# An mLSTM cell without its decay matrix: values divided by the decay, scores under a triangle

## The chip, the cores and the metric

The kernel runs on one core of one Trainium2 chip. Its time is device microseconds of one execution; the figure that counts is the median of several executions. Five engines work side by side and meet at semaphores: TensorE (PE in the profile, its weight loads apart as PEld), VectorE (DVE), ScalarE (ACT), GpSimd (POOL) and SyncE (SP), which here only issues DMAs. PE's results land in PSUM; POOL works on SBUF alone.

## The reference

An mLSTM cell over 4 batches, 8 heads, 768 tokens and head size 40, and then a dense pair of layers of 320 x 2048 and 2048 x 320 over the 3072 tokens, with g = h - tanh(h) between them.

```python
for t in range(S):
    m_new = np.maximum(f_gate[:, :, t] + m, i_gate[:, :, t])
    f_stab = np.exp(f_gate[:, :, t] + m - m_new)
    i_stab = np.exp(i_gate[:, :, t] - m_new)
    m = m_new
    C = f_stab * C + i_stab * outer(vt, kt)
    n = f_stab * n + i_stab * kt
    h_tilde = C @ qt
    denom = np.maximum(np.abs(n . qt), 1.0)
    y[:, :, t] = sigmoid(o_gate[:, :, t]) * h_tilde / denom
...
h = x @ w_in
g = h - np.tanh(h)
return (g @ w_out).astype(np.float32)
```

The forget gates are drawn as 3 + 0.5 x normal, the input gates as 0.5 x normal. `w_in` and `w_out` are float64 (a float32 array times a numpy float64), so each weight is 8 bytes in memory and is turned into float32 on the chip.

## The kernel before

**Units.** The 768 tokens are cut into 6 chunks of L = 128. A unit is one chunk of one batch with its 8 heads: 24 units, numbered chunk by chunk (unit n is chunk n // 4 of batch n % 4). Within a chunk the recurrence is written as attention. For each head PE multiplies keys and queries into scores (`score`, into the PSUM tile `ps`), DVE multiplies the scores by a decay matrix (L393, into `E`), and PE multiplies the result by the scaled values `vs` (`intra`, into `ph`). What comes from earlier chunks is added by `inter`: the queries times the decay since the chunk's start (`qg`) times the carried state. `update` forms the chunk's contribution to the state (`pc`), `gate` divides by the denominator and applies the output gate (`ys`), and `turn` transposes the unit's result into `xT`, the input of the dense layers. The denominator is a column of ones' product: `vs` carries exp(i - m) as its 41st column, so column D of `ph` is n . q.

**The decay matrix.** For each pair (s, t) of a chunk it holds the product of the forget factors between s and t. Each unit loads its 8 rows of forget factors from `f_rows`, spread over 128 partitions (`fetch`, a 512 KB DMA), and one scan over 128 x 1024 elements (L362) turns them, with `diag` as the added operand, into the products. `qg` comes from `g_rows`, the running product from the chunk's start, by two more DMAs, and POOL multiplies it by the queries (L378). Both tables of rows are made at the start: L233 to L242 compute exp of the log decays with a polynomial on DVE, PE transposes the result (L247), DVE scans it (L255), and ACT's queue writes both to memory (L258, L259).

**The start.** Two scans' worth of gate work on 32 rows (L203 to L208) gives m, the log decays `lf` and i - m. PE transposes `lf` and i - m into columns, and two matmuls over a triangle and over ones (L218 to L227) give the decay to the chunk's end (`eS`) and of a whole chunk (`eT`). `ei` holds exp(i - m), and that times `eS`.

**Weights.** 40 blocks of `w_in` and `w_out` (8 column pairs p, five blocks for each) are loaded as 8-byte words (L283) and turned into float32 by five DVE operations (L293, L296, L304, L305, L306) and two ACT operations (L294, L297). `convert` lists the steps; each p has a due time, the first dense item that needs it.

**Dense items.** Two units make a group g of 256 tokens; 12 groups and 8 pairs p make 96 items. `up` multiplies (12 recorded matmul passes into `ph_up`), ACT squares twice, DVE forms `gt` with two operations (L501, L502), and `down` of the item two places earlier multiplies by `w_out` (8 recorded passes into `po`). The first four groups are taken in parts, as `STAGES` says: an entry (g, first, last) runs pairs first to last of group g, and the number beside a list is how many cell slots are spread over it. Partial sums go to `part`.

**Cell slots.** A slot (s, o, x) is the scores of unit s, the value matmuls, update and gate of unit o, and the transpose of unit x, interleaved step by step. `begin` in a slot prepares unit o (`vs` on POOL), issues the loads for unit s + 1 and runs the decay scan for unit s. The first four slots run before the dense items, with the first nine conversion steps merged in. `kz` (keys) has two buffers, `q2` (queries) three.

**Order.** The order of PE's instructions is written by hand: class `T` chains each to the one before. The other engines are in the order that the framework gives them. All loads go through SP's queue, the outputs and the two tables of rows through ACT's.

**The branch.** The dense layers use a short polynomial for h - tanh(h), good while squares stay small. ACT adds up the squares in `sums`; at the end (L606 to L611) the maximum is compared with `TINY`, and only if it is larger, everything is computed a second time with a full formula.

Of the kernel before, what the change touches and what calls it, by code (L numbers as in the profile page):

```python
# [47 lines left out]
TINY = 0.0224  # L49

# [11 lines left out]
def kernel(  # L62
# [16 lines left out]
    class T:  # L79
# [60 lines left out]
    f_sb = att.tile([BH, S], FP, name="f_sb", tag="E", bufs=4)  # L140
    i_sb = att.tile([BH, S], FP, name="i_sb", tag="E", bufs=4)
# [7 lines left out]
    q2 = [const.tile([128, HH, L], FP, name=f"q2{i}") for i in range(3)]  # L149
    for t in (kz[0], q2[0], kz[1], q2[1], q2[2]):  # L150
        V.memset(t, 0.0)
# [3 lines left out]
    def load_unit(n):  # L155
        c, b = divmod(n, B)
        t = ld[n] = {"kz": kz[n % 2], "q2": q2[n % 3]}
        for i in range(2):
            r0, heads = i * D, slice(i, H, 2)
            nc.sync.dma_start(out=t["kz"][r0:r0 + D, heads], in_=kT[b, c, :, heads])  # L160
            nc.sync.dma_start(out=t["q2"][r0:r0 + D], in_=qT[b, c, :, heads])  # L161
        for name, src, bufs in (("v", v, 3), ("k", k, 4), ("o", o_gate, 4)):
            t[name] = load.tile([L, H, D], FP, name=name, tag=name, bufs=bufs)
            nc.sync.dma_start(out=t[name], in_=src[b, c])
# [5 lines left out]
    after = const.tile([128, 128], FP, name="after")  # L170
    ones = const.tile([128, TOP], FP, name="ones")
# [17 lines left out]

    G.memset(after, 1.0)  # L190
    G.affine_select(out=after, in_=after, compare_op=OP.is_ge, fill=0.0, base=-1,
                    pattern=[[-1, 128]], channel_multiplier=1)
    G.tensor_copy(out=diag, in_=ident.unsqueeze(1).to_broadcast([128, H, L]))
# [3 lines left out]
    ei = const.tile([L, 2, NT, BH], FP, name="ei")  # L197
# [3 lines left out]
    m_sb = att.tile([BH, S], FP, name="m_sb", tag="E", bufs=4)  # L201
    lf = att.tile([BH, S], FP, name="lf", tag="E", bufs=4)
    V.tensor_tensor_scan(out=m_sb, data0=f_sb, data1=i_sb, initial=-1.0e30, op0=OP.add, op1=OP.max)  # L203

    V.memset(lf[:, 0:1], 0.0)
    V.tensor_tensor(out=lf[:, 1:S], in0=f_sb[:, 1:S], in1=m_sb[:, 0:S - 1], op=OP.add)
    V.tensor_tensor(out=lf[:, 1:S], in0=lf[:, 1:S], in1=m_sb[:, 1:S], op=OP.subtract)
    V.tensor_tensor(out=i_sb, in0=i_sb, in1=m_sb, op=OP.subtract)  # L208

    def to_columns(row):  # L210
        p = ps_b.tile([L, NT, BH], FP, name="pcol", tag="b")
        for c in range(NT):
            T.transpose(p[:, c, :], row[:, c * L:(c + 1) * L], ident[0:BH, 0:BH])
        return p

    V.tensor_copy(out=lfT, in_=to_columns(lf))
    A.activation(out=ei[:, 0], in_=to_columns(i_sb), func=AF.Exp)
    for w in (after, ones):  # L218
        p = ps_b.tile([w.shape[1], NT, BH], FP, name="psum_lf", tag="b")
        T.matmul(p.rearrange("p c n -> p (c n)"), w, lfT.rearrange("p c n -> p (c n)"),  # L220
                 start=True, stop=True)
        if w is after:
            A.activation(out=eS, in_=p, func=AF.Exp)
            continue
        half = p.rearrange("p c (b j two) -> p (c b) two j", two=2, j=HH)
        A.activation(out=eT, in_=half[:, :, 1, :], func=AF.Exp)
        A.activation(out=eT[0:D], in_=half[0:D, :, 0, :], func=AF.Exp)  # L227
    V.tensor_tensor(out=ei[:, 1], in0=ei[:, 0], in1=eS, op=OP.mult)


    NR = NT * BH // 2
    xr, n, f = (mlp.tile([L, 2, NR], FP, name=name, tag=tag) for name, tag in (("xr", "z"), ("n", "z"), ("f", "q")))
    V.tensor_single_scalar(xr, lfT.rearrange("p (i c) n -> p i (c n)", i=2), -87.0, op=OP.max)  # L233
    V.tensor_scalar(out=n, in0=xr, scalar1=1.4426950408889634, scalar2=ROUND, op0=OP.mult, op1=OP.add)
    V.tensor_single_scalar(n, n, ROUND, op=OP.subtract)
    for part in LN2:
        V.scalar_tensor_tensor(out=xr, in0=n, scalar=-part, in1=xr, op0=OP.mult, op1=OP.add)
    V.tensor_single_scalar(f, xr, EXPO[0], op=OP.mult)
    for coef in EXPO[1:]:
        V.scalar_tensor_tensor(out=f, in0=f, scalar=coef, in1=xr, op0=OP.add, op1=OP.mult)  # L240
    V.tensor_scalar(out=n.bitcast(I32), in0=n, scalar1=127.0, scalar2=float(1 << 23), op0=OP.add, op1=OP.mult)
    V.scalar_tensor_tensor(out=f, in0=f, scalar=1.0, in1=n, op0=OP.add, op1=OP.mult)  # L242


    row = ps_b.tile([NR, 2, L], FP, name="row", tag="b")
    for i in range(2):
        T.transpose(row[:, i, :], f[:, i, :], ident)  # L247
    frow = mlp.tile([NR, 2, L], FP, name="frow", tag="q")
    grow = mlp.tile([NR, 2, L], FP, name="grow", tag="gt", bufs=LAG + 2)
    zero = mlp.tile([NR, L], FP, name="zero", tag="gt", bufs=LAG + 2)  # L250
    V.memset(zero, 0.0)
    V.memset(frow[:, :, 0:1], 0.0)
    V.tensor_copy(out=frow[:, :, 1:L], in_=row[:, :, 1:L])
    for i in range(2):
        V.tensor_tensor_scan(out=grow[:, i, :], data0=row[:, i, :], data1=zero, initial=1.0, op0=OP.mult, op1=OP.add)  # L255
    f_rows = dram.tile([2, NR, L], FP, name="f_rows")
    g_rows = dram.tile([2, NR, L], FP, name="g_rows")
    nc.scalar.dma_start(out=f_rows.rearrange("i r t -> r i t"), in_=frow)  # L258
    nc.scalar.dma_start(out=g_rows.rearrange("i r t -> r i t"), in_=grow)  # L259

    def spread(dst, rows, n, heads):

        i, r = divmod(n * H, NR)
        nc.sync.dma_start(out=dst, in_=rows[i:i + 1, r:r + H, :][:, heads, :].to_broadcast(list(dst.shape)))
# [4 lines left out]
    for c, (_, rows) in enumerate(KC):  # L269
        if rows < 128:  # L270
            G.memset(w_in[:, c, :], 0.0)

    def weights(dst, src):
# [4 lines left out]
        def fetch():  # L278
            if src.dtype == FP:
                nc.sync.dma_start(out=dst, in_=src)  # L280
                return
            w["st"] = conv.tile([128, n], I64, name="w64", tag="w64", bufs=8)[0:p]
            nc.sync.dma_start(out=w["st"], in_=src)  # L283
# [28 lines left out]
    def convert():  # L312

        blocks = []
        for p in range(NP):
            cols = slice(p * WB, (p + 1) * WB)
            for c, (r0, rows) in enumerate(KC):
                blocks.append(weights(w_in[0:rows, c, cols], moe_w_in[r0:r0 + rows, cols]))
            for f in (2 * p, 2 * p + 1):
                blocks.append(weights(w_out[:, f, :], moe_w_out[f * 128:(f + 1) * 128, :]))  # L320
# [10 lines left out]
    xT = [const.tile([128, NK, TG], FP, name=f"xT{i}") for i in range(NX)]  # L331
    part = [const.tile([L, DM], FP, name=f"part{i}") for i in range(FIRST * GT)]

    qg = [const.tile([128, HH, L], FP, name=f"qg{i}") for i in range(3)]
    ys = [const.tile([L, NK * 128], FP, name=f"ys{i}") for i in range(2)]
    state = [[const.tile([128, HH, 2, D1], FP, name=f"state{b}_{i}") for i in range(2)] for b in range(B)]
    for t in xT + qg + ys + sum(state, []):
# [9 lines left out]
    def fetch(n):  # L347
        load_unit(n)
        t = ld[n]
        t["E"] = att.tile([L, H, L], FP, name="E", tag="E", bufs=4)  # L350
        spread(t["E"], f_rows, n, slice(0, H))

    def decay(n):
# [3 lines left out]
        if t["c"]:  # L357
            t["qg"] = qg[n % 3]
            for i in range(2):
                spread(t["qg"][i * D:(i + 1) * D], g_rows, n, slice(i, H, 2))  # L360
        row = t["E"].rearrange("p h t -> p (h t)")
        V.tensor_tensor_scan(out=row, data0=row, data1=diag.rearrange("p h t -> p (h t)"), initial=0.0,  # L362
                             op0=OP.mult, op1=OP.add)

    def prepare(n):
# [11 lines left out]
        if t["c"]:  # L377
            G.tensor_tensor(out=t["qg"][0:TOP], in0=t["qg"][0:TOP], in1=t["q2"][0:TOP], op=OP.mult)  # L378
# [7 lines left out]
    def score(n, h):  # L386
# [4 lines left out]
        if h % HH == HH - 1:  # L391
            P = t["E"][:, h - HH + 1:h + 1, :]
            V.tensor_tensor(out=P, in0=t["ps"], in1=P, op=OP.mult)  # L393

    def inter(n, j):
# [3 lines left out]
        if t["c"]:  # L401
            T.matmul(pair(t["ph"], j), t["qg"][:, j, :], pair(state[t["b"]][t["c"] % 2].rearrange("p j two d -> p (j two) d"), j), start=(j == 0), stop=False,
                     skip_group_check=True)

    def intra(n, h):
        t = un[n]
        T.matmul(t["ph"][:, h, :], t["E"][:, h, :], t["vs"][:, 0, h, :], start=(t["c"] == 0 and h == 0), stop=True,
                 skip_group_check=True)

    def gate(n):  # L410
# [4 lines left out]
        V.tensor_scalar(out=den, in0=ph[:, :, D], scalar1=-1.0, scalar2=1.0, op0=OP.mult, op1=OP.max)  # L415
# [31 lines left out]
    def cell_slot(s, o, x):  # L447
# [4 lines left out]
        def begin():  # L452
# [4 lines left out]
            if s is not None:  # L457
                if s + 1 < NU:
                    fetch(s + 1)
                decay(s)  # L460

        steps.append((0.0, begin))
# [18 lines left out]
    sums = const.tile([128, NG * NP], FP, name="sums")  # L481
# [68 lines left out]

    slots = [(0, None, None), (1, 0, None), (2, 1, 0), (3, 2, 1), (4, 3, 2), (5, None, 3), (6, 4, None)]
# [158 lines left out]
```

## Time and profile before

| | us |
|---|---|
| median of 3 runs | 656.22 |
| lowest, highest | 655.97, 657.41 |
| the profiled execution, its own time | 656.12 |
| its span, first to last instruction | 654.1 |

| engine | busy, us | share of the span |
|---|---|---|
| PE, matmul | 601.2 | 92% |
| PEld, weight load | 499.9 | 76% |
| DVE | 367.9 | 56% |
| ACT | 211.1 | 32% |
| POOL | 90.4 | 14% |

A row of the groups reads: line, engine, operation, output <- inputs, sizes, count | busy us, mean ns of one | idle time of that engine just before them, and whom it waited for. A row of the timeline reads: start, length, engine, line, operation, count, and in brackets the idle time before it and what ended it. SPq and ACTq are DMA issues in the queues of SP and ACT. A row of the waits reads: who waited for whom, us in total, times, longest.

### The profile page before, as it was taken

The numbers are of one execution on the slowest core, as the hardware profiler recorded it, in microseconds if no ns is written. First come the engines' busy times: TensorE is split into PE (matmuls) and PEld (weight loads), VectorE is DVE, ScalarE is ACT, GpSimd is POOL, SyncE is SP. The second block draws the span as 40 slices with busy tenths as digits, with TensorE's granted clock in tenths as the row PEclk, the third lists the DMA queues.
The fourth block names the chain that finished last, engine by engine and source line by source line (L and its number), as shares of the span: only waits on it lengthen the run. The fifth ranks groups of instructions, "written<-read, shape, count | busy, mean of one in ns | idle before, by whom it ended". The sixth has DMA issues, their size and how long they took to land.

```text
span 654.1 us, 8562 instructions
## 1 busy us (share of the span) xinstructions
PE 601.2 (92%) x3100; PEld 499.9 (76%) x3100; DVE 367.9 (56%) x697; ACT 211.1 (32%) x471; POOL 90.4 (14%) x90
## 2 busy tenths in 40 slices
PE   1376879999899999999999999999999999999994
PEld 1376758778788888888888888888888888878773
DVE  8797999999962356556436436435433332322231
ACT  2222464346422322222232232232232232242321
POOL 7412303310220102202202201101101000000000
PEclk9878888999999999999999999999999999999999
DMA  5548547462320112223212214112100000000000
GB/s 161 174 128 257 183 140 208 142 194 91 103 74 0 60 34 92 92 83 92 71 44 92 72 43 123 63 41 74 53 30 11 0 22 1 0 21 0 22 1 26
DMA packets 46212, 50.98 MB, mean 78 GB/s; under 512 B 3985, under 2 KB 38417, under 8 KB 46161
## 3 DMA queue, kind: packets, MB, share of 16 engines
q1 hardware_dynamic: 42288, 46.22, 23.1%
q10 hardware_dynamic: 3872, 4.13, 1.9%
q8 instruction: 26, 0.43, 0.3%
q14 instruction: 26, 0.20, 0.1%
HBM read 46.20 MB, written 4.13 MB: 77 GB/s over the span
## 4 chain that ended last, share of the span: by engine, by line
PE 80%; DVE 11%; DMA 3%; issue 3%; SPq 1%; POOL 1%; ACT 0%; ACTq 0%; DVEq 0%; POOLq 0%
PE ph_up L92 35%; PE po L92 30%; PE ph L92 6%; PE ps L92 5%; PE pc L92 2%; DMA E<-f_rows 2%; DVE E L362 2%; DVE w_e L305 1%; PE px L96 1%; DVE w_m L296 1%; DVE w_e L293 1%; DVE w_r L304 1%; DVE gt L501 1%; SPq L161 1%; DVE E L393 1%
## 5 line engine op out<-in xcount | busy, mean ns | idle before, releaser
L92 PE MATMUL ph_up<-xT,w_in 128*128 128x256 f32 x1152 | 314.0, 392 | 2.6 <-ACT xT L444 1.1
L92 PE MATMUL po<-w_out,gt 128*128 128x320 f32 x768 | 253.2, 443 | 4.0 <-DVE part L520 4.0
L92 PEld LDWEIGHTS ph_up<-xT,w_in 128*128 128x128 f32 x1152 | 200.5, 192 | 29.9 <-ACT xT L444 2.4
L501 DVE SCALAR_TENSOR_TENSOR gt<-ph_up,z 128x512 f32<-128x512 f32 x96 | 66.1, 688 | 202.7 <-ACT z L499 202.7
L92 PEld LDWEIGHTS po<-w_out,gt 128*128 128x128 f32 x768 | 132.9, 192 | 33.4 <-DVE part L520 4.9
L499 ACT ACTIVATE z<-ph_up 128x512 f32<-128x512 f32 x96 | 57.2, 596 | 248.8 <-PE ph_up L92 248.8
L92 PEld LDWEIGHTS ps<-q,kz 128*128 128x128 f32 x384 | 70.7, 207 | 20.4 <-DVE E L393 9.0
L92 PE MATMUL ps<-q,kz 128*128 128x128 f32 x384 | 76.6, 297 | 8.7 <-DVE E L393 8.7
L92 PEld LDWEIGHTS ph<-vs,E 128*128 128x128 f32 x384 | 69.5, 201 | 10.7 <-issue 0.8
L502 DVE SCALAR_TENSOR_TENSOR gt<-q,gt 128x512 f32<-128x512 f32 x96 | 67.6, 705 | 6.6 <-ACT q L500 1.0
L500 ACT ACTIVATE q<-z,tiny 128x512 f32<-128x512 f32 x96 | 69.2, 721 | 2.8
L362 DVE TENSOR_TENSOR_SCAN E<-E,diag 128x1024 f32<-128x1024 f32 x24 | 54.7, 2283 | 12.1 <-DMA E<-f_rows 12.1
L92 PE MATMUL ph<-vs,E 128*128 128x41 f32 x384 | 59.8, 254 | 0.6 <-ACT xT L444 0.6
L375 POOL TENSOR_TENSOR vs<-v,ei 128x640 f32<-128x640 f32 (+1 forms) x24 | 31.0, 1295 | 151.1 <-PE ph L92 128.0
L393 DVE TENSOR_TENSOR E<-ps,E 128x512 f32<-128x512 f32 x48 | 32.9, 687 | 26.9 <-PE ps L92 26.6
L382 POOL TENSOR_TENSOR state<-state,eT 80x328 f32<-80x328 f32 x16 | 13.2, 823 | 208.7 <-DVE state L433 143.6
L92 PEld LDWEIGHTS ph<-state,qg 128*128 128x128 f32 x160 | 29.7, 192 | 10.5 <-issue 2.3
L378 POOL TENSOR_TENSOR qg<-qg,q 80x512 f32<-80x512 f32 x20 | 31.6, 1582 | 42.2 <-DMA qg<-g_rows 38.5
L92 PEld LDWEIGHTS pc<-vs,k 128*80 128x80 f32 x160 | 22.0, 161 | 15.1 <-DVE ys L420 4.4
L92 PE MATMUL pc<-vs,k 128*80 128x82 f32 x160 | 24.2, 250 | 7.0 <-DVE ys L420 4.0
L92 PE MATMUL ph<-state,qg 128*128 128x82 f32 x160 | 28.1, 258 | 1.5 <-issue 1.5
L297 ACT ACTIVATE w_r<-w 128x256 f32<-128x256 uint32 (+2 forms) x40 | 18.3, 460 | 32.3 <-DVE w_in L306 16.6
(88 smaller groups left out, 312.3 us busy)
## 6 DMA issues: line engine op xcount, KB each, us to landing
E<-f_rows SPq DMA_DIRECT2D x24, 512.0 KB
w<-in_moe_w_out SPq DMA_DIRECT2D x16, 320.0 KB
w<-in_moe_w_in SPq DMA_DIRECT2D x16, 256.0 KB
kz<-in_kT SPq DMA_DIRECT2D x48, 80.0 KB
q<-in_qT SPq DMA_DIRECT2D x48, 80.0 KB
v<-in_v SPq DMA_DIRECT2D x24, 160.0 KB
k<-in_k SPq DMA_DIRECT2D x24, 160.0 KB
o<-in_o_gate SPq DMA_DIRECT2D x24, 160.0 KB
```

Source lines behind the costliest of these rows:

```text
L92: return cls.keep(nc.tensor.matmul(*args, **kwargs))
L96: return cls.keep(nc.tensor.transpose(*args, **kwargs))
L297: A.activation(out=r.bitcast(FP), in_=lo, func=AF.Copy, scale=2.0 ** -52)
L362: V.tensor_tensor_scan(out=row, data0=row, data1=diag.rearrange("p h t -> p (h t)"), initial=0.0, op0=OP.mult, op1=OP.add)
L375: G.tensor_tensor(out=t["vs"][:, both, :, 0:D], in0=t["v"].unsqueeze(1).to_broadcast(shape), in1=scale.unsqueeze(3).to_broadcast(shape), o ...
L378: G.tensor_tensor(out=t["qg"][0:TOP], in0=t["qg"][0:TOP], in1=t["q2"][0:TOP], op=OP.mult)
L382: G.tensor_tensor(out=new, in0=old, in1=eT[:, n, :].unsqueeze(2).to_broadcast([TOP, HH, 2 * D1]), op=OP.mult)
L393: V.tensor_tensor(out=P, in0=t["ps"], in1=P, op=OP.mult)
L499: A.activation(out=z, in_=ph, func=AF.Square, accum_out=sums[:, g * NP + p:g * NP + p + 1])
L500: A.activation(out=q, in_=z, func=AF.Square, bias=tiny)
L501: V.scalar_tensor_tensor(out=gt, in0=ph, scalar=TINY_POLY[0], in1=z, op0=OP.mult, op1=OP.mult)
L502: V.scalar_tensor_tensor(out=gt, in0=q, scalar=TINY_POLY[2], in1=gt, op0=OP.add, op1=OP.mult)
```

## The change

With F[t] the product of the forget factors from the chunk's start to t, the decay between s and t is F[t] / F[s]. The change puts the two factors in other places. The values, with their column for the denominator, are scaled by exp(i - m) / F[s] (`ei[:, 0]`, with `inv` = 1/F from a third small matmul over the triangle `upto`). The scores are multiplied by the triangle `upto` alone, the same for every unit. The common factor F[t] cancels between numerator and denominator, if the bound 1 in the denominator becomes 1/F[t] (`inv`, in `gate`). So `inter` uses the plain queries, and `E`, `qg`, `diag` and both tables of rows are gone from the main path. F must not be too small: the smallest log of F goes into a new column of `sums`, and the branch at the end runs if it lies below `DEEP` = -12; the branch still has the decay matrix and now makes the tables itself.

Around it: the gates' work becomes a function `gates`, called after slot 0; `f_sb`, `i_sb`, `m_sb` and `lf` lie in `xT` tiles; `xT` is not cleared any more; `q2` has four buffers; the weight loads of the first pair p go through ACT's queue; every slot is (s, s - 1, s - 2), and `STAGES` lists the first groups in another order.

```diff
-        ([(0, 2, 2), (1, 2, 2)], 1),
-        ([(0, 3, 3), (1, 3, 3)], 2),
-        ([(2, 0, 3)], 0),
-        ([(0, 4, 4), (1, 4, 4), (2, 4, 4)], 2),
-        ([(3, 0, 4)], 0),
-        ([(0, 5, 6), (1, 5, 6), (2, 5, 6), (3, 5, 6)], 2),
-        ([(0, 7, 7), (1, 7, 7), (2, 7, 7), (3, 7, 7)], 1),
+        ([(0, 2, 2), (1, 2, 2)], 2),
+        ([(2, 0, 2)], 0),
+        ([(0, 3, 3), (1, 3, 3), (2, 3, 3)], 2),
+        ([(3, 0, 3)], 0),
+        ([(0, 4, 4), (1, 4, 4), (2, 4, 4), (3, 4, 4)], 1),
+        ([(0, 5, 6), (1, 5, 6), (2, 5, 6), (3, 5, 6)], 1),
+        ([(0, 7, 7), (1, 7, 7), (2, 7, 7), (3, 7, 7)], 2),
...
-    q2 = [const.tile([128, HH, L], FP, name=f"q2{i}") for i in range(3)]
+    q2 = [const.tile([128, HH, L], FP, name=f"q2{i}") for i in range(4)]
...
+        A.activation(out=ei[:, 2], in_=to_columns(i_sb), func=AF.Exp)
+        for w in (upto, after, ones):
...
+            if w is upto:
+                V.tensor_single_scalar(inv, p, 2 * DEEP, op=OP.max)
+                V.tensor_reduce(out=sums[:, NG * NP:], in_=inv.rearrange("p c n -> p (c n)"), axis=mybir.AxisListType.X, op=OP.min)
+                A.activation(out=inv, in_=inv, func=AF.Exp, scale=-1.0)
+                V.tensor_single_scalar(sums[:, NG * NP:], sums[:, NG * NP:], TINY / DEEP, op=OP.mult)
+                continue
...
+        for i, w in enumerate((inv, eS)):
+            V.tensor_tensor(out=ei[:, i], in0=ei[:, 2], in1=w, op=OP.mult)
...
+            queue = nc.sync if p else nc.scalar
...
-        row = t["E"].rearrange("p h t -> p (h t)")
-        V.tensor_tensor_scan(out=row, data0=row, data1=diag.rearrange("p h t -> p (h t)"), initial=0.0,
-                             op0=OP.mult, op1=OP.add)
+        t["P"] = att.tile([L, H, L], FP, name="P", tag="P", bufs=4)
+        t["qs"] = t["q2"]
...
-        if t["c"]:
-            G.tensor_tensor(out=t["qg"][0:TOP], in0=t["qg"][0:TOP], in1=t["q2"][0:TOP], op=OP.mult)
...
-            V.tensor_tensor(out=P, in0=t["ps"], in1=P, op=OP.mult)
+            V.tensor_tensor(out=P, in0=t["ps"], in1=P if t.get("decays") else upto.unsqueeze(1).to_broadcast([L, HH, L]),
+                            op=OP.mult)
...
-        V.tensor_scalar(out=den, in0=ph[:, :, D], scalar1=-1.0, scalar2=1.0, op0=OP.mult, op1=OP.max)
+        V.scalar_tensor_tensor(out=den, in0=ph[:, :, D], scalar=-1.0, in1=inv[:, t["c"], t["hs"]], op0=OP.mult, op1=OP.max)
...
-    slots = [(0, None, None), (1, 0, None), (2, 1, 0), (3, 2, 1), (4, 3, 2), (5, None, 3), (6, 4, None)]
+    slots = [tuple(n if 0 <= n < NU else None for n in (s, s - 1, s - 2)) for s in range(NU + 2)]
...
-    slots += [tuple(n if n < NU else None for n in (s, s - 2, s - 3)) for s in range(len(slots), NU + 3)]
...
     for i in range(AHEAD):
+        if i == 1:
+            gates()
         merge(cell_slot(*slots[i]), first[i * len(first) // AHEAD:(i + 1) * len(first) // AHEAD])
```

More of the change, by code (lines that the diff above doesn't have):

```diff
@@ L137 @@
     ps_b = ctx.enter_context(tc.tile_pool(name="ps_b", bufs=2, space=PSUM))
-    f_sb = att.tile([BH, S], FP, name="f_sb", tag="E", bufs=4)
-    i_sb = att.tile([BH, S], FP, name="i_sb", tag="E", bufs=4)
+    xT = [const.tile([128, NK, TG], FP, name=f"xT{i}") for i in range(NX)]
+    f_sb, i_sb, m_sb, lf = (t.rearrange("p k t -> p (k t)")[0:BH, 0:S] for t in xT[-4:])
     nc.sync.dma_start(out=f_sb, in_=f_gate)
@@ L170 @@
     after = const.tile([128, 128], FP, name="after")
+    upto = const.tile([128, 128], FP, name="upto")
     ones = const.tile([128, TOP], FP, name="ones")
@@ L202 @@
[L202 to L256, printed above, removed]
@@ L345, in pair, with begin @@
         return t[:, 2 * j:2 * j + 2].rearrange("p two d -> p (two d)")
[L347 to L353, printed above, removed]
+    def begin(n):
         t = un[n] = ld.pop(n)
@@ new lines, in spread, with begin_any @@
+    def spread(dst, rows, n, heads):
+        i, r = divmod(n * H, NR)
+        nc.sync.dma_start(out=dst, in_=rows[i:i + 1, r:r + H, :][:, heads, :].to_broadcast(list(dst.shape)))
+    def begin_any(n):
+        begin(n)
+        t = un[n]
+        spread(t["P"], f_rows, n, slice(0, H))
+        row = t["P"].rearrange("p h t -> p (h t)")
+        V.tensor_tensor_scan(out=row, data0=row, data1=diag.rearrange("p h t -> p (h t)"), initial=0.0,
+                             op0=OP.mult, op1=OP.add)
+        t["decays"] = True
+        if t["c"]:
+            t["qs"] = att.tile([128, HH, L], FP, name="qs", tag="P", bufs=4)
+            V.memset(t["qs"], 0.0)
+            for i in range(2):
+                spread(t["qs"][i * D:(i + 1) * D], g_rows, n, slice(i, H, 2))
+            V.tensor_tensor(out=t["qs"], in0=t["qs"], in1=t["q2"], op=OP.mult)
```

115 lines of the change are left out of this document (79 added, 36 removed).

## The prediction, made before the changed kernel was run

> **What bounds the kernel now.** I read the page's busy times and slices first, then cut the span where the slices change.
>
> ```profile
> PE 601.2 (92%) x3100; PEld 499.9 (76%) x3100; DVE 367.9 (56%) x697; ACT 211.1 (32%) x471; POOL 90.4 (14%) x90
> PE   1376879999899999999999999999999999999994
> DVE  8797999999962356556436436435433332322231
> ```
>
> PE is busy 92% of the span, but not in the first ten of its slices, and there DVE is at 9. An average of 56% for DVE hides that it is full early and half empty later. The next view is the busy time by stretch. Its cuts are events: 31.35 is the second unit's first score matmul, 55.61 the first `ph_up` matmul, 89.35 a `ph_up` matmul that waited for weights, 182.90 the square that follows the 16th `ph_up` tile, 639.17 the last `po` group. Columns: length, then busy time with its count for each engine, granted clock, DMA share, GB/s.
>
> ```profile
> 0.00:31.35 31.35, 7.08 (x35) 6.12 (x35) 25.25 (x51) 8.04 (x16) 19.18 (x33) 0.92 0.53 162
> 31.35:55.61 24.26, 18.41 (x126) 17.59 (x126) 22.77 (x45) 6.30 (x16) 5.00 (x5) 0.82 0.57 172
> 55.61:89.35 33.74, 27.41 (x131) 23.32 (x131) 31.20 (x67) 15.87 (x38) 7.08 (x5) 0.85 0.59 184
> 89.35:182.90 93.55, 85.29 (x481) 71.65 (x482) 91.23 (x216) 43.65 (x103) 20.46 (x15) 0.96 0.51 154
> 182.90:639.17 456.27, 456.27 (x2305) 376.80 (x2304) 195.76 (x315) 135.02 (x296) 38.71 (x32) 1.00 0.14 45
> 639.17:654.10 14.93, 6.74 (x27) 4.45 (x25) 1.70 (x5) 2.26 (x5) 0.00 (x0) 0.90 0.09 29
> ```
>
> From 182.90 to 639.17 PE has no idle time and a clock of 1.00: nothing that DVE, POOL or the DMAs lose there changes the end. All that can be won lies before 182.90, where PE idles 24.3 + 5.9 + 6.3 + 8.3 = 44.8 us and its busy time is stretched by the lower clock. DVE is busy 94%, 92% and 98% of stretches two to four: DVE is what PE waits for there. The start is a chain of its own:
>
> ```profile
> 4.74 1.74 DVE L203 TENSOR_TENSOR_SCAN m_sb<-f_sb,i_sb 32x768 f32<-32x768 f32 x1
> 10.23 0.82 PE L96 MATMUL pcol<-ident,lf 32*128 32x32 f32 x6 [10.23 <-DVE zero L251]
> 12.66 0.33 ACT L223 ACTIVATE eS<-psum_lf 128x192 f32<-128x192 f32 x1 [0.61 <-PE psum_lf L92]
> 18.61 0.63 PE L96 MATMUL row<-ident,f 128*96 128x128 f32 x2 [5.35 <-DVE f L242]
> 19.03 3.62 PE L92 MATMUL ps<-q,kz 128*128 128x128 f32 x16
> 19.37 3.87 POOL L375 TENSOR_TENSOR vs<-v,ei 128x640 f32<-128x640 f32 x3
> 19.73 0.35 ACTq L258 DMA_DIRECT2D f_rows<-frow  x1
> 28.21 2.29 DVE L362 TENSOR_TENSOR_SCAN E<-E,diag 128x1024 f32<-128x1024 f32 x1 [2.49 <-DMA E<-f_rows]
> 31.35 1.22 PE L92 MATMUL ps<-q,kz 128*128 128x128 f32 x4 [8.69 <-DVE E L393]
> ```
>
> PE's order is written by hand, so the scores of unit 0 stand behind the transpose of the polynomial's result (18.61). Then come the write of `f_rows` (19.73), its read back into `E`, the scan (28.21) and the product with the scores, for which PE waits 8.69 us until 31.35.
>
> **The change part by part.** The rows of what goes and of what stays:
>
> ```profile
> L362 DVE TENSOR_TENSOR_SCAN E<-E,diag 128x1024 f32<-128x1024 f32 x24 | 54.7, 2283 | 12.1 <-DMA E<-f_rows 12.1
> L378 POOL TENSOR_TENSOR qg<-qg,q 80x512 f32<-80x512 f32 x20 | 31.6, 1582 | 42.2 <-DMA qg<-g_rows 38.5 <-DMA q<-in_qT 2.4 <-DMA E<-f_rows 1.3
> L393 DVE TENSOR_TENSOR E<-ps,E 128x512 f32<-128x512 f32 x48 | 32.9, 687 | 26.9 <-PE ps L92 26.6
> L375 POOL TENSOR_TENSOR vs<-v,ei 128x640 f32<-128x640 f32 (+1 forms) x24 | 31.0, 1295 | 151.1 <-PE ph L92 128.0 <-DMA v<-in_v 12.6 <-ACT o L384 5.8
> L415 DVE TENSOR_SCALAR den<-ph 128x8 f32<-128x8 f32 x24 | 3.9, 161 | 18.1 <-PE ph L92 18.0
> ```
>
> Removed from the main path: 24 scans (54.7 us of DVE), 20 `qg` products (31.6 us of POOL), 24 `E` loads of 512 KB and 40 `qg` loads with their places in SP's queue, the exponential's polynomial and the write and read of `f_rows`. Kept at its price: L393 still reads one operand from PSUM and one from SBUF, now `upto`; 48 x 687 ns. L415 turns into an operation of two tensors of 128x8: between its own 161 ns and the 0.47 us of the 128x320 product at L420 (row below), so at most 24 x 0.3 = 7 us of DVE, spread over all units; I take nothing, since 54.7 us leave the same engine. Added once: the `upto` matmul (ACT waited 0.61 us for the like one with `after`, row at 12.66), a maximum, a minimum, an exponential and a product over 128x192, each near the 0.33 us of that row. The matmuls of units and of the dense layers keep count and shape, so stretch five is worth zero either way.
>
> **Term 1, the start.** PE now does unit 0's scores before the gates. Its loads need these issues and this landing time:
>
> ```profile
> 4.67 0.76 SPq L161 DMA_DIRECT2D q<-in_qT  x1
> 6.48 0.43 SPq L164 DMA_DIRECT2D o<-in_o_gate  x1
> 9.50 0.47 ACT L384 ACTIVATE o<-o 128x320 f32<-128x320 f32 x1 [7.42 <-DMA o<-in_o_gate]
> ```
>
> The last `q` of unit 0 is issued by 5.43; with the 2.6 us from 6.91 to 9.50 it has landed by 8.0. The 16 score passes took 3.62 us: 11.6. From the first transpose (10.23) to the end of the row at 12.66 took 2.8 us; with the added matmul and four small operations, 0.61 + 4 x 0.33 = 1.9 less what ACT and DVE do side by side, about 1.5, that is 15.9. `vs` (1.3 us; POOL isn't held by the `xT` and `qg` memsets any more) ends at 17.3, and unit 0's value matmuls start at 17.5. Before, they were free to go at 31.35. **-13.9 us.** Bounds: if DVE takes the scores' product ahead of the gates' scan and subtractions (5.5 us between 4.74 and the transposes at 10.23), 23 and -8.4; if the transposes overlap loads better, 15 and -16.4.
>
> **Term 2, 31.35 to 55.61, units 1 to 3.** PE's waits in this stretch:
>
> ```profile
> PE pc L92 <- issue: 2.9, 1, 2.9
> PE px L96 <- DVE state L435: 0.9, 1, 0.9
> PE pc L92 <- DVE ys L420: 0.8, 1, 0.8
> PE ph L92 <- ACT xT L444: 0.6, 1, 0.6
> 42.44 0.47 DVE L420 TENSOR_TENSOR ys<-ph,o 128x320 f32<-128x320 f32 x1
> E<-f_rows SPq DMA_DIRECT2D x24, 512.0 KB
> ```
>
> The four sum to 5.2 us, and behind the 2.9 stands `ys` at 42.44, late behind weight conversion and unit 2's rows on DVE. Three scans (6.75 us) leave DVE's 22.77. What is late next: `kz` has two buffers, so a unit's load waits for the scores two units back, and its seven issues (4 x 0.76 and 3 x 0.43 by the rows of term 1) take SP 4.3 us plus landing, some 6 us per unit: 18 at least. Between 18 and 24.3 I take 20.3, near PE's own 18.41. **-4.0** (0 to -6.3). The weights' first five loads move to ACT's queue: about 0.4 us of issue each on an engine busy a quarter of this time; behind them wait its copies, at most 2 us, inside the bound.
>
> **Term 3, 55.61 to 89.35.** DVE: 31.20, three scans in it by the first row below; PE's waits follow.
>
> ```profile
> 55.61:89.35 33.74, 6.80 (x3) 0.85 0.59 184
> 89.35:182.90 93.55, 11.40 (x5) 0.96 0.51 154
> PE px L96 <- DVE ys L420: 2.7, 1, 2.7
> PE pc L92 <- DVE ys L420: 2.7, 1, 2.7
> 76.85 1.34 POOL L378 TENSOR_TENSOR qg<-qg,q 80x512 f32<-80x512 f32 x1 [3.01 <-DMA qg<-g_rows]
> L296 DVE TENSOR_SCALAR w_m<-w 128x256 int32<-128x256 int32 (+2 forms) x40 | 15.1, 378 | 0.0
> 76.99 1.35 DVE L296 TENSOR_SCALAR w_m<-w 128x256 int32<-128x256 int32 x1
> ```
>
> L296's mean is 378 ns, and 1.35 us beside the `qg` product: each such product can hold DVE a microsecond. DVE's need falls to 31.2 - 6.8 - 1 = 23.4, under PE's 27.41. So PE binds, with a rest of waits for the second and third weight blocks, whose due times here don't move: 28.5. **-5.2** (0, if the weights' loads bind, to -8.7).
>
> **Term 4, 89.35 to 182.90.** Five scans and some five holds, 16 us, leave 75 of DVE's 91 against PE's 85.29. The new table also wants the fourth weight block before item 9 instead of 6 and the fifth before 16 instead of 12. Of 8.3 us of idle time I count 6: **-6.0** (-2 to -10, the clock's part included).
>
> Sum: -13.9 - 4.0 - 5.2 - 6.0 = -29.1. The profiled execution took 656.12, its span 654.1; the median of the runs is 656.22. 656.2 - 29.1 = **627.1**. The bounds give 656.2 - 10.4 = 645.8 and 656.2 - 41.4 = 614.8.
>
> The granted clock was 0.82 and 0.85 in stretches two and three, and 1.00 later. The Trainium skill, TensorE: Matmul & The Clock Gate, in the part on the HAM clock gate, says that the array runs at half rate until about 3.4 us of work have passed, and falls back after as long an idle window. By that rule the wait from 11.6 to about 13 and again to 17.5 makes unit 1 start cold, and shorter gaps after it keep the array warm: terms 2 and 3 would come out some 5 us better. The trace agrees with the fall (four score passes took 1.22 us at 31.35, behind an idle stretch, and 0.65 us at 37.15, row below); whether the gaps stay short no run here shows.
>
> ```profile
> 37.15 0.65 PE L92 MATMUL ps<-q,kz 128*128 128x128 f32 x4
> ```
>
> **The rivals.** (a) *PE never waits again after 17.5 and runs at full clock*: busy times by their clocks from 31.35 on, 18.41 x 0.82 + 27.41 x 0.85 + 85.29 x 0.96 + 456.27 + 6.74 x 0.90 = 582.6, plus 17.5, the tail's 8.2 idle and 2.0 outside the span: 610. For it: DVE's need falls under PE's in each stretch. Against: weights are due early and one chain of PSUM buffers passes through DVE. Chance 0.22, 606 to 617.
>
> (b) *Weight conversion and loads still bind*: terms 3 and 4 give only their small ends, and the start the in-order 23: -8.4 - 2 - 2 - 2 = 642. For it: DMA share 0.59 in stretch three, DVE at 97 to 100%. Against: 512 KB per unit leave the DMAs. Chance 0.19, 637 to 650.
>
> (c) *Slower: the unit's value matmuls now stand one slot after its scores for every unit.* PE's order is fixed, so `vs` and the masked scores must be ready, or PE stops in stretch five, which has no slack. If each of 22 slots waited for L375 and L393, 1.3 + 0.7 = 2.0 us, that is 44 us against 29 won: 671. It decides from 1.3 us per slot on. Against: units 0 to 3 already ran so, and PE's waits in stretches two and three name no POOL. Chance 0.04.
>
> (d) *The branch at the end is taken*, since F falls below its bound; PE's work would run again, over 1200. Forget gates are drawn around 3, so the running maximum follows them and the log decay stays at 0. Chance 0.01. No change: 0.02.
>
> **How the numbers follow.** Forecast 617 to 637: 0.52. Range 608 to 645: it leaves out a part of (a) and (b), and (c), (d). Faster by over 0.2% (about what a measurement here can tell from none) 0.93, within 0.02, slower 0.05.
>
> **What would show it.** First value matmul near 17.5; first `ph_up` matmul near 38; DVE below 90% from 40 on; no PE wait for `vs` or L393 later; PE idle-free from about 155, then the same 456 us to the last `po` group. A first value matmul after 25, or any PE idle after 200, makes the prediction wrong.

## The result, and the profile after

The changed kernel takes 622.21 us, median of 4 runs (620.52 to 623.99), the kernel before 656.58 beside it: a ratio of 0.9476, 95% interval 0.9438 to 0.9514. The forecast was 627.1 with a range of 608 to 645. By the medians the change won 34.4 us. The profiled execution took 623.99, the longest of the four, and its span is 622.3; the traces below are of that one.

The page's busy times and slices of the changed kernel:

```profile
PE 594.7 (96%) x3100; PEld 496.8 (80%) x3100; DVE 307.7 (49%) x663; ACT 214.0 (34%) x475; POOL 55.2 (9%) x62
PE   3779999999999999999999999999999999999995
DVE  8789999995344535543434434333343332322231
```

DVE lost 60 us of work, and PE is full from the fourth slice instead of the twelfth. The busy time by stretch follows, first three stretches of before, then the changed kernel. The cuts are the same events in both: the first value matmul (`ph<-vs`), the first `ph_up` matmul, the square behind the 16th `ph_up` tile, and in the changed kernel a place near the end.

```profile
0.00:32.36 32.36, 8.09 (x38) 7.13 (x39) 26.25 (x52) 8.50 (x17) 19.18 (x33) 0.91 0.54 165
32.36:55.61 23.25, 17.40 (x123) 16.58 (x122) 21.76 (x44) 5.83 (x16) 5.00 (x5) 0.84 0.55 167
55.61:182.90 127.29, 112.70 (x611) 94.97 (x612) 122.43 (x282) 59.52 (x139) 27.54 (x20) 0.93 0.53 162
```

```profile
0.00:21.03 21.03, 6.84 (x38) 6.09 (x39) 19.02 (x43) 12.40 (x24) 12.46 (x25) 0.89 0.70 196
21.03:45.32 24.29, 20.32 (x122) 19.59 (x123) 18.28 (x47) 8.78 (x22) 5.74 (x6) 0.67 0.47 144
45.32:150.89 105.57, 102.90 (x595) 87.97 (x596) 97.60 (x261) 57.49 (x133) 18.17 (x14) 1.00 0.45 133
150.89:607.00 456.11, 456.11 (x2312) 377.15 (x2311) 171.11 (x309) 133.04 (x295) 18.78 (x19) 1.00 0.09 28
```

The first stretch is 11.3 us shorter, the second 1.0 longer, the third 21.7 shorter. The last holds no idle time in either kernel. At the 16th tile the changed kernel is 32.0 us ahead, at the end of the span 31.8. So the whole gain lies before that tile.

Length alone misleads, as the two kernels don't do the same cells in each stretch. So I use **lost time**: a stretch's length less what its recorded matmul passes take at full pace. The prices come from two rows of the changed kernel's chain of waits late in the span (start, length, group, passes):

```profile
563.67 2.59 PE ph_up L97 x12
566.26 2.15 PE po L97 x8
```

That is 0.216 us a pass of `ph_up` and 0.269 of `po`; for the small ones, 0.11 and for `pc` 0.09, half of the 0.22 and 0.18 in `cell_slot`'s list of costs. In the start only the 20 score passes count as work. Lost time by stretch (the last column ends at the last square):

| | start | units 1 to 3 | to the 16th tile | rest |
|---|---|---|---|---|
| before | 30.2 | 10.3 | 24.0 | 1.6 |
| changed | 18.8 | 11.4 | 4.1 | 1.4 |

The second stretch is the surprise: DVE has 18.28 us of work in 24.29 there, 75%, and the stretch is no shorter. PE is busy 20.32 of 24.29, with a granted clock of 0.67. Two weight-load rows of the timeline show the pace, one from this stretch and one from a little later:

```profile
33.70 0.98 PEld L97 LDWEIGHTS ps<-q,kz 128*128 128x128 f32 x4
37.58 0.53 PEld L97 LDWEIGHTS ps<-q,kz 128*128 128x128 f32 x4
```

The same four loads take 0.98 us and then 0.53. PE starts its value matmuls at half pace at 21.03 and keeps it until about 37. The pace had fallen before the wait that ends there; the four loads ahead of it are slow already:

```profile
16.34 0.99 PEld L97 LDWEIGHTS ps<-q,kz 128*128 128x128 f32 x4
```

The list of waits below puts the wait at 21.03 down to POOL's `vs`, whose product for unit 0 had run since 17.90. Run e9 shows that PE waited for the last of these rows, on ACT:

```profile
17.25 0.23 ACT L245 ACTIVATE eT<-psum_lf 80x96 f32<-80x96 f32 x1
17.50 1.28 ACT L354 ACT_TABLE_LOAD   x1
18.80 0.47 ACT L354 ACTIVATE o<-o 128x320 f32<-128x320 f32 x1
19.28 1.28 ACT L246 ACT_TABLE_LOAD   x1
20.58 0.24 ACT L246 ACTIVATE eT<-psum_lf 40x96 f32<-40x96 f32 x1
20.73 0.42 ACT L346 COPY vs<-ei 128x16 f32<-128x16 f32 x3
```

A sigmoid was ordered between two exponentials, each switch loads a table, and the copy of `vs`'s last column stands behind both.

The groups that took the place of those shown of before, and all of PE's waits in the execution (who, for whom: us, times, longest):

```profile
L363 DVE TENSOR_TENSOR P<-ps,upto 128x512 f32<-128x512 f32 x48 | 32.9, 686 | 36.5 <-PE ps L97 35.7 <-POOL state L321 0.3
L347 POOL TENSOR_TENSOR vs<-v,ei 128x640 f32<-128x640 f32 (+1 forms) x24 | 32.5, 1359 | 173.8 <-PE ph L97 162.5 <-DMA v<-in_v 6.6 <-DVE ei L248 3.9
L386 DVE SCALAR_TENSOR_TENSOR den<-ph,inv 128x8 f32<-128x8 f32 x24 | 3.9, 161 | 10.3 <-PE ph L97 10.2
```

```profile
PE ps L97 <- DMA q<-in_qT: 9.8, 1, 9.8
PE ph L97 <- POOL vs L347: 3.4, 1, 3.4
PE pc L97 <- DVE ys L391: 2.0, 3, 1.4
PE ph_up L97 <- ACT xT L415: 1.7, 3, 0.6
PE pc L97 <- issue: 1.5, 1, 1.5
PE px L101 <- DVE state L404: 0.9, 1, 0.9
PE psum_lf L97 <- DVE lfT L229: 0.9, 1, 0.9
PE ph L97 <- ACT xT L415: 0.4, 1, 0.4
```

The product under the triangle costs what the product with the decay matrix did (686 and 687 ns), and the denominator with a second tensor 161 ns as before. Behind the 9.8 us in which the first unit's loads land, PE waits 10.8 us in all. By this list it waits for POOL once, at 21.03, and never for the masked scores.

### The profile page after: what moved, and what is told of

It reads as the page before. It is cut to its first block, busy times and chain, and to the rows that moved or that the text cites. A ratio compares the mean times of both kernels' runs of the same rounds, so it can differ in the third digit from the quotient of the medians.

```text
span 622.3 us, 8351 instructions
## 1 busy us (share of the span) xinstructions
PE 594.7 (96%) x3100; PEld 496.8 (80%) x3100; DVE 307.7 (49%) x663; ACT 214.0 (34%) x475; POOL 55.2 (9%) x62
## 4 chain that ended last, share of the span: by engine, by line
PE 92%; DVE 3%; POOL 1%; issue 1%; DMA 1%; ACT 0%; ACTq 0%; SPq 0%; DVEq 0%
PE ph_up L97 41%; PE po L97 34%; PE ph L97 7%; PE ps L97 6%; PE pc L97 2%; PE px L101 1%; DMA w<-in_moe_w_in 1%; DVE P L363 1%; DVE w_e L277 0%; POOL vs L347 0%; DVE q L157 0%; DVE kz L157 0%; POOL w_in L255 0%; POOL own L194 0%; DVE w_in L290 0%
## 5 line engine op out<-in xcount | busy, mean ns | idle before, releaser
L97 PE MATMUL ph_up<-xT,w_in 128*128 128x256 f32 x1152 | 307.4, 387 | 1.7 <-ACT xT L415 1.7
L97 PE MATMUL po<-w_out,gt 128*128 128x320 f32 x768 | 249.8, 441 | 0.0
L97 PEld LDWEIGHTS ph<-vs,P 128*128 128x128 f32 x384 | 69.6, 201 | 16.7 <-POOL vs L347 3.7
L97 PE MATMUL ph<-vs,P 128*128 128x41 f32 x384 | 60.5, 254 | 3.8 <-POOL vs L347 3.4
L363 DVE TENSOR_TENSOR P<-ps,upto 128x512 f32<-128x512 f32 x48 | 32.9, 686 | 36.5 <-PE ps L97 35.7
L347 POOL TENSOR_TENSOR vs<-v,ei 128x640 f32<-128x640 f32 (+1 forms) x24 | 32.5, 1359 | 173.8 <-PE ph L97 162.5
L97 PEld LDWEIGHTS ph<-state,q 128*128 128x128 f32 x160 | 28.8, 190 | 6.1 <-ACT xT L415 0.3
L97 PE MATMUL ph<-state,q 128*128 128x82 f32 x160 | 28.1, 257 | 0.0
L278 ACT ACTIVATE w_e<-w_e,rebias 128x256 int32<-128x256 int32 (+2 forms) x40 | 20.9, 526 | 8.8 <-DVE w_e L277 8.2
L404 DVE SCALAR_TENSOR_TENSOR state<-pc,own,state 80x164 f32<-80x164 f32 x32 | 11.3, 379 | 19.5 <-PE pc L97 19.3
```

The lines of the kernel that those rows point to most:

```text
L97: return cls.keep(nc.tensor.matmul(*args, **kwargs))
L278: A.activation(out=e, in_=e, func=AF.Relu, scale=8.0, bias=rebias[0:p])
L347: G.tensor_tensor(out=t["vs"][:, both, :, 0:D], in0=t["v"].unsqueeze(1).to_broadcast(shape), in1=scale.unsqueeze(3).to_broadcast(shape), o ...
L363: V.tensor_tensor(out=P, in0=t["ps"], in1=P if t.get("decays") else upto.unsqueeze(1).to_broadcast([L, HH, L]), op=OP.mult)
L404: V.scalar_tensor_tensor(out=new, in0=pc, scalar=own[0:TOP, i:i + 1], in1=new, op0=OP.mult, op1=OP.add)
```

## The experiments

Twelve kernels ran. Ten are the changed kernel with something put back or moved, e10 is the kernel before with the new order, and e12 is e6 with added work. Ratios are to the kernel before on the same chip (its median 654.8 to 656.4 there), with 95% intervals. Differences in us are to the 622.21 above, although the kernel before varies by 1.7 us from chip to chip. Lost time by stretch is as above, from one profiled execution each.

| run | median, us | ratio | start | units 1 to 3 | to the 16th tile |
|---|---|---|---|---|---|
| e1_old_order | 625.52 | 0.9546 [0.9504, 0.9589] | 19.5 | 10.1 | 4.9 |
| e2_scan_back | 650.86 | 0.9931 [0.9890, 0.9971] | 25.7 | 12.8 | 12.0 |
| e3_loads_back | 628.64 | 0.9576 [0.9541, 0.9610] | 18.9 | 11.1 | 6.7 |
| e4_pool_back | 629.16 | 0.9587 [0.9547, 0.9628] | 19.0 | 13.9 | 7.0 |
| e5_all_back | 663.56 | 1.0111 [1.0073, 1.0149] | 25.7 | 16.6 | 25.0 |
| e11_scan_behind_product | 638.47 | 0.9743 [0.9713, 0.9774] | 21.1 | 14.8 | 13.4 |
| e13_chain_back | 642.12 | 0.9793 [0.9764, 0.9822] | 22.1 | 13.7 | 16.8 |
| e10_before_new_order | 652.97 | 0.9951 [0.9924, 0.9978] | 30.4 | 11.8 | 21.0 |
| e6_gates_first | 618.79 | 0.9431 [0.9394, 0.9468] | 16.9 | 5.3 | 6.1 |
| e8_warm | 620.12 | 0.9433 [0.9398, 0.9467] | 19.5 | 5.7 | 4.9 |
| e9_copy_pool | 622.09 | 0.9484 [0.9445, 0.9523] | 17.5 | 10.2 | 4.2 |
| e12_gates_first_warm | 630.66 | 0.9627 [0.9597, 0.9657] | 23.3 | 8.6 | 3.5 |

(In e8 and e12 the added matmuls of constants are not counted as work.)

**The order or the engines' load?** The first run takes back the order alone.

```diff
-    slots = [tuple(n if 0 <= n < NU else None for n in (s, s - 1, s - 2)) for s in range(NU + 2)]
+    slots = [(0, None, None), (1, 0, None), (2, 1, 0), (3, 2, 1), (4, 3, 2), (5, None, 3), (6, 4, None)]
...
-        ([(0, 2, 2), (1, 2, 2)], 2),
+        ([(0, 2, 2), (1, 2, 2)], 1),
...
```

> The changed kernel (622.2 us) with the old STAGES table and the old list of slots. Theory D (VectorE was the bound from 31 to 183 us; taking the scans and the POOL products off it is what won the stretches after the first ph_up matmul): the order is worth little, 622 to 627. Rival O (the new order, with later due times of weight blocks and units one slot nearer, won those stretches): about 15 to 20 us come back, 637 to 642.

Measured: 625.52, 3.3 us more. The other way round, the new order in the kernel before:

> The kernel before (656.6 us) with the new STAGES table and the new list of slots, and nothing else. Theory D: VectorE still bounds, only the later due times of two weight blocks help: 651 to 657. Rival O: 10 to 20 us faster, 637 to 647.

Measured: 652.97, 3.1 us less than the 656.08 beside it. Both ways agree: the order is worth about 3 us (1.4 to 5.0 by e10's interval), and rival O falls.

**DVE's scans.** Each slot gets a scan on a scratch tile that nobody reads.

```diff
                 begin(s)
+                row = junk[s % 2].rearrange("p h t -> p (h t)")
+                V.tensor_tensor_scan(out=row, data0=row, data1=row, initial=0.0, op0=OP.mult, op1=OP.add)
```

> The changed kernel with a scan of 128x1024 on a scratch tile in each slot, whose result nobody reads: VectorE's 24 x 2.28 us are back, the wait for them is not. Theory D: VectorE is busy 28.0 of 29.2 us and 69.6 of 76.4 in the two stretches after the first ph_up matmul, so the scans there overfill it: +8 to +14, 630 to 636. Rival O: within 3 of 622.

Measured: 650.86, 28.6 more, beyond either theory. With no input to wait for, the scans were placed early. On DVE's timeline one stands at 16.25 and two follow at 19.02, ahead of the product that gives `ei`, which comes at 24.05. Later one pile-up stops PE in the stretch that otherwise has no idle time; from the waits of this run, 167 to 640 us:

```profile
PE po L97 <- DVE part L494: 8.9, 1, 8.9
```

So this run shows a misplaced scan, not the old one's price. A scan that reads its own unit's product can't run ahead:

```diff
             V.tensor_tensor(out=P, in0=t["ps"], in1=..., op=OP.mult)
+            if h == H - 1 and not t.get("decays"):
+                V.tensor_tensor_scan(out=junk..., data0=t["P"]..., data1=t["P"]..., initial=0.0, op0=OP.mult, op1=OP.add)
```

> The changed kernel with the scan's 2.28 us of VectorE in a place of its own: for each unit a scan of 128x1024 that reads the unit's masked scores behind their second product and writes a scratch tile, so that it can't run ahead of its unit (in e2_scan_back scans ran ahead in bunches, before the gates and once before an eviction) and nothing waits for its result. Theory D (VectorE's time itself): +8 to +12, 630 to 634. Rival B (e2_scan_back lost by the bunches alone): within 3 of 622.

Measured: 638.47, 16.3 more. Rival B falls, and theory D's price was too low. The stretches show why. From the windows of this run, cut as before:

```profile
23.29:51.04 27.75, 19.79 (x122) 19.02 (x122) 21.40 (x46) 7.66 (x20) 11.51 (x7) 0.85 0.48 144
51.04:165.89 114.85, 110.30 (x595) 94.45 (x596) 109.43 (x260) 56.74 (x132) 27.14 (x14) 0.93 0.39 117
51.04:60.00 8.96, 8.96 (x39) 8.35 (x39) 6.88 (x15) 2.22 (x5) 2.98 (x2) 0.50 0.52 162
```

DVE is back at 95% of the long stretch (109.43 of 114.85), and the granted clock at 0.93, as before the change; without the scans it was 1.00. DVE is nearly full without the scans too, 97.60 of 105.57 us or 92%: some 8 us were free, and the scans bring 11.8. PE does the same 595 passes and is busy 7.4 us longer with them, which is what the clock gives (102.90 / 0.93 = 110.6). So of the 9.3 us that the stretch loses, 1.9 are idle time and 7.4 pace. The pace falls behind a wait: one of 3.17 us for `ys` ends at 45.63, and from 47.95 four passes of scores take 1.06 to 1.20 us, until at 59.97 they take 0.65. From 51.04 to 60.00 PE has no gap and a clock of 0.50. POOL does the same 14 instructions in 27.14 us instead of 18.17. Its timeline beside DVE's:

```profile
53.21 0.81 POOL L354 TENSOR_TENSOR state<-state,eT 80x328 f32<-80x328 f32 x1
61.23 1.26 POOL L349 TENSOR_TENSOR vs<-v,ei 128x640 f32<-128x640 f32 x1 [7.20 <-PE ph L97]
61.56 3.07 DVE L368 TENSOR_TENSOR_SCAN junk<-P 128x1024 f32<-128x1024 f32 x1
62.44 2.71 POOL L354 TENSOR_TENSOR state<-state,eT 80x328 f32<-80x328 f32 x1
```

The state's product takes 0.81 us with no scan beside it and 2.71 beside the scan, and ends half a microsecond after it; the scan takes 3.07 instead of 2.28, having begun beside `vs`. In these rows the two engines take turns. This agrees with the Trainium skill, SBUF — State Buffer, in its part on SBUF's two separate sides: GpSimd and a VectorE operation with two SBUF inputs exclude each other for a whole instruction.

**The loads and the wait for them.** A 512 KB load per unit that nobody reads, on SP's queue:

```diff
+                    nc.sync.dma_start(out=junk[(s + 1) % 2], in_=qT[b, c, 0:1].to_broadcast([128, H, L]))
```

> The changed kernel with a 512 KB broadcast load per unit into a scratch tile on SP's queue, which nobody reads: the 12 MB of E loads are back. Theory D: within 2 of 622. Rival L (the E loads held up the loads of weights and units): +5 to +10, 627 to 632.

Measured: 628.64, 6.4 more (2.1 in the profiled execution, whose third stretch lost 2.6 more). Theory D said at most 2; rival L's time holds at its lower end. Its mechanism is likely and not shown: PE's waits in this run name no load behind the first unit's, but in the third stretch ACT waits 5.2 us for weight loads, and in the changed kernel not at all. The loads' part was not in my sum. Next the whole chain, without POOL's product: load, scan in place, then the product over it.

```diff
+                    ld[s + 1]["P"] = att.tile([L, H, L], FP, name="P", tag="P", bufs=4)
+                    nc.sync.dma_start(out=ld[s + 1]["P"], in_=qT[b, c, 0:1].to_broadcast([128, H, L]))
+                if s:
+                    row = un[s]["P"].rearrange("p h t -> p (h t)")
+                    V.tensor_tensor_scan(out=row, data0=row, data1=row, initial=0.0, op0=OP.mult, op1=OP.add)
```

> The changed kernel with the whole old chain ahead of each product from unit 1 on: a 512 KB broadcast load into the unit's P tile one slot early, a scan in place, then the product, which writes over it. No POOL product. Theory D: the scan's time and the load's wait stand in VectorE's order, +14 to +22, 636 to 644. Rival W (a wait for the load costs nothing beyond the scan's own time): as e11_scan_behind_product, within 3.

Measured: 642.12, 19.9 more, within theory D's range, and 3.7 more than e11, too near rival W's 3 to decide. The wait isn't what this run shows: DVE waits 12.6 us in all for these loads, but 12.1 of it behind 170 us, where DVE's waits cost the end nothing, and none in the third stretch. There the 3.4 us more than in e11 are near the 2.6 that the unread loads of e3 cost.

**POOL's product.**

```diff
+                if s >= B:
+                    G.tensor_tensor(out=qj[0:TOP], in0=qj[0:TOP], in1=q2[s % 4][0:TOP, :, 0:L - 2], op=OP.mult)
```

> The changed kernel with one POOL product of 80x504 on a scratch tile for each unit after the fourth. Theory D: each can hold one VectorE operation for about 1 us; some six of them fall before the 16th item: +1 to +4, 623 to 626. Rival: POOL has the time, within 1 of 622.

Measured: 629.16, 7.0 more, beyond both. The third stretch lost 2.9 us more, inside theory D's 1 to 4. Units 1 to 3 lost 2.5 more, at a clock of 0.56. They have no such product, but those for units 4 and 5 ran ahead into their stretch. Three rows of this run's timeline:

```profile
30.64 1.20 POOL L435 TENSOR_TENSOR qj<-qj,q 80x504 f32<-80x504 f32 x1
30.74 1.44 DVE L391 TENSOR_TENSOR o<-o,den 128x320 f32<-128x320 f32 x1
33.02 0.81 PE L97 MATMUL pc<-vs,k 128*80 128x82 f32 x4 [2.84 <-issue]
```

DVE's product takes 1.44 us there instead of the changed kernel's 0.48, on the way to the `ys` that ends just before 33.02. After the wait of 2.84 us PE goes on at half pace. How much of the 2.5 comes from this isn't settled.

**All of it together,** which leaves PE waiting for none of the results:

> The changed kernel with the scratch load, the scratch scan on it and a POOL product of 80x504 for each unit after the fourth: the engines' load of before is back, but no matmul waits for any of it. Theory D: +12 to +18, 634 to 640, with the rest of the way to 656 being the start's chain, about 11 us, and the waits for the scans. Rival O: within 5 of 622.

Measured: 663.56, slower than before the change. The third stretch loses 25.0 us, against 24.0 in the kernel before, as much as the change won there. But the likeness is no proof, since the unread scans run ahead as in e2: two of them stand before the product that gives `ei` at 24.52, and the start lost 6.9 more; twelve stand between 187 and 229 us, and the part behind the 16th tile lost about 8 more. The range had room for neither. DVE waited for the loads for 2.9 us in all.

**The start and the clock.** Gates before slot 0:

```diff
-        if i == 1:
+        if i == 0:
             gates()
```

> The changed kernel with the gates ahead of slot 0, so that PE's transposes of the log decays stand before unit 0's scores as in the kernel before. Theory S1 (the start won by the round trip through f_rows and the polynomial alone): within 1 of 622. Rival S2 (the new place of unit 0's scores in PE's order won part of it): +2 to +4.

Measured: 618.79, 3.4 less: both theories missed the sign. In the profiled executions the new place of unit 0's scores cost time. The windows and one row of the timeline of this run:

```profile
0.00:19.16 19.16, 7.97 (x39) 6.85 (x40) 16.08 (x40) 10.89 (x22) 12.59 (x25) 1.00 0.67 190
19.16:37.38 18.22, 13.64 (x124) 12.86 (x122) 16.70 (x43) 4.95 (x14) 5.88 (x6) 1.00 0.54 164
19.49 0.53 PEld L97 LDWEIGHTS ps<-q,kz 128*128 128x128 f32 x4
```

The scores now fill PE's wait for `vs`, the clock is 1.00, and units 1 to 3 take 18.22 us instead of 24.29. The start is 1.9 us shorter too, and there ACT's order changed along with the gates: the first copy of `vs`'s column, at 16.68, stands ahead of the next table load, at 17.01. The other way to fill that wait is work for nobody, eight matmuls of constants behind the gates' own:

```diff
+            for x in range(8):
+                T.matmul(idle[:, 0, 0:128], ident, upto, start=True, stop=True)
```

> The changed kernel with eight 128x128 matmuls of constants after the gates' matmuls, into a PSUM tile that is not used yet, so that PE is at work while it waits for vs. In the changed kernel the clock granted from 21.03 to 45.32 us was 0.67, and that stretch is as long as before. Theory C (the half clock is what kept units 1 to 3 from getting shorter): clock above 0.85 there, 3 to 7 us faster, 615 to 619. Rival K (key loads through two buffers, or VectorE, set the pace of the units): the clock rises and the time stays within 2 of 622.

Measured: 620.12, 2.1 less. The second stretch of this run:

```profile
21.80:40.31 18.51, 15.44 (x122) 14.58 (x122) 17.10 (x46) 7.96 (x20) 5.82 (x6) 0.91 0.50 148
```

The clock is 0.91 and the length 18.51: theory C holds for the stretch. The medians show less than its 3 us, as rival K had it, and the two intervals overlap. The four runs of the changed kernel go the same way: the two with mean clocks of 0.991 and 0.995 took 620.58 and 620.52, the two with 0.982 took 623.84 and 623.99. That is a hint only, as e3's four runs do not: 629.72 us at 0.994, 626.13 at 0.981.

> The changed kernel with the 41st column of unit 0's vs copied by POOL instead of ACT. In the changed kernel ACT loads two tables (17.50 and 19.28 us) before that copy at 20.73, and the first value matmul follows at 21.03, while POOL's product for unit 0 had run since 17.90. Theory T (the table loads hold the first value matmul): it starts 1 to 2 us earlier, 620 to 621.5. Rival: it stays at 21, because POOL's products finish then, and the time stays.

With `G.tensor_copy` for unit 0's column the first value matmul came at 19.66, 1.4 us earlier; the median, 622.09, is unchanged:

```profile
19.66 0.64 PE L97 MATMUL ph<-vs,P 128*128 128x41 f32 x4 [1.76 <-POOL vs L347]
```

The table loads did hold that matmul, as theory T said, but its time didn't follow: 1.4 us there is less than the spread of the runs (621.03 to 627.86).

> The kernel of e6_gates_first (618.8 us) with 16 matmuls of the identity by itself ahead of everything on PE, into a PSUM tile that is not used yet: PE is at work from about 1.5 us and its clock should be granted before the first transposes at 10 us. Theory C (the clock of the first units sets the spread of e6_gates_first, 617.3 to 621.0, and of the changed kernel, 620.5 to 624.0): 614 to 617.5 with less spread. Rival K: 617 to 620, as without them.

Measured: 630.66, against both. The 16 matmuls ended at 6.75, 3.1 us before the gates' transposes, and the cause is elsewhere. From the waits of PE:

```profile
PE psum_lf L97 <- DVE lfT L229: 5.9, 1, 5.9
```

The framework's order of DVE changed with PE's new work: the copy of the log decays, at 11.52 us in e6, moved behind weight conversion to 16.20, though its input, the transposes, begins at 9.84 and in e6 at 9.97; the first value matmul came at 25.58 instead of 19.16. The clock theory can't be read from this run. Of the 12 us between the two medians, the 6.4 that the start lost in the profiled executions hang on an order of DVE that nobody wrote down. The best version is e6_gates_first; its interval and the changed kernel's overlap from 0.9438 to 0.9468, so 3 us is its median's lead and not a proven one. Not tried: the first weights back on SP's queue.

## Why the prediction held

| term | forecast | measured, in lost time |
|---|---|---|
| 1, the start | -13.9 | -11.4 |
| 2, units 1 to 3 | -4.0 | +1.1 |
| 3 and 4, to the 16th tile | -11.2 | -19.9 |
| the rest | 0 | -0.2 |
| sum | -29.1 | -30.4 |

The sum of lost time is 1.4 us short of the spans' 31.8; that much lies in the tail, from the last square to the end of the span. That the total came so near is in part luck: term 1 fell short by 2.5, term 2 by 5.1 and with the wrong sign, and terms 3 and 4 won 8.7 more than forecast.

**Term 1** named the right chain, as far as the two timelines tell: no run puts the round trip through `f_rows` back. Its first value matmul was put at 17.5 and came at 21.03: the step "`vs` ends at 17.3" left out ACT's copy of the 41st column behind two table loads. That is 1.4 of the 3.5 us (e9); the gates also ended later, with `ei` ready at 17.81 where the sum had 15.9. The second bound, the scan in DVE's queue behind the scores' product, didn't occur: the gates' DVE work ended at 9.81, beside the first score at 9.75.

**Term 2** failed at the step that put the stretch near PE's own 18.41 us: that number was busy time at a clock of 0.82, and the changed kernel got 0.67. The waits went as said, the pace got worse. The paragraph on the clock gate said that unit 1 would start cold, and it did, although the pace fell before the last wait (the loads at 16.34). But the paragraph had the array warm from then on, which left a few microseconds cold; it was some 16. e6 and e8 show what the forecast lacked: at clocks of 1.00 and 0.91 the stretch is 18.22 and 18.51 long. The first `ph_up` matmul, expected near 38, came at 45.32.

**Terms 3 and 4** are under-sized by 8.7 us. That DVE's time is the largest cause is shown: with the scans back (e11) the stretch loses 9.3 of the 19.9 us again. With the loads too (e13) it loses 12.7. I priced the relief by PE's idle time, 11 of 14.6 us, and that part was right: the idle time fell from 14.6 to 2.7, by 11.9. The mis-sized part is the clock's, the other 8.0. The clock of the stretch rose from 0.93 to 1.00 once PE had few gaps left. By cause, two sizes were missing: the loads, for which I took nothing beyond room in SP's queue (2.6 of lost time, 6.4 in the median), and POOL's product (2.9), of which I took a microsecond in term 3 and a share in term 4. The pieces put back one by one (e11, e3, e4, and 0.8 for the order in e1) give 15.6 of the 19.9; the other 4.3 no single run shows. The sign that DVE would fall below 90% from 40 on didn't come before the 16th tile: it is busy 102.73 of the 110.89 us from 40.00 to 150.89, 93%. DVE stayed nearly full there and only stopped being what PE waits for.

**Stretch five** was right to 0.2 us: no DVE time saved there counts, and 12 of the 24 scans stood there. **Rival (c)** fell: PE waits for `vs` once, for 3.4 us at the start, and never for the masked scores behind 151 us. **Rival (a)**, 606 to 617, was right about the third stretch, which lost only 4.1 us, and wrong about the second, where the clock was 0.67. **Rival (b)**, 637 to 650, fell with that stretch; its DMA share was 0.45. The branch was not taken.

## What to carry to other kernels

Cut the span where the bound changes, and price each engine's relief in its own stretch: 54.7 us of scans went, and only those in front of the 16th tile counted. Where the engine at the bound is waited for by PE, its relief is worth more than PE's idle time, since the gaps also lower PE's clock (11.9 us of idle time and 8.0 of pace here). When work is moved to shorten a start, look at what PE does while it waits: here the shorter chain left PE idle at the wrong moment, and in the profiled executions the old place of the scores was better.

## What the runs showed of the hardware

- PE ran at half pace from 21.03 to about 37 us in the changed kernel, 16 us, although it was busy 20.32 of 24.29 us there; before the change, after 8.7 idle microseconds, the pace rose within 6 (1.22 us for four passes at 31.35, 0.65 at 37.15). The Trainium skill, TensorE: Matmul & The Clock Gate, in the part on the HAM clock gate, has the full rate come after about 3.4 us of work; the runs differ from it, and why this stretch stayed slow so long is open.
- A table load between an exponential and a sigmoid takes 1.28 us, with the next operation right behind it (17.50 to 18.80); two of them on ACT held the first value matmul by 1.4 us (e9).
